# Chunk attention and a token-mixing MLP in one kernel: the hand-written order of its steps and of its loads is replaced by another

## The chip, the core and the metric

One core of a Trainium2 chip runs the whole kernel. The engines work from queues of their own and in the order of the program: PE (TensorE) multiplies and transposes, DVE (VectorE) and ACT (ScalarE) read its results out of the eight PSUM banks, POOL (GpSimd) issues the loads and SP (SyncE) nearly all stores. The time is the device time of one execution in microseconds; the median of the runs counts.

## What is computed

Inputs q, k and v have 8 batches, 8 heads, 576 tokens and 64 numbers a head. Attention stays within chunks of 64 tokens:

```python
scores = scale * np.matmul(q_c, k_c.transpose(0, 1, 2, 4, 3))
scores = scores - np.max(scores, axis=-1, keepdims=True)
attn = np.exp(scores)
attn = attn / (np.sum(attn, axis=-1, keepdims=True) + 1e-09)
out = np.matmul(attn, v_c)
```

Its result x has 512 columns for a token. The second half mixes tokens over the whole sequence of 576, with two small weight matrices, and multiplies by an output matrix of 512 x 512:

```python
wq = x @ w_q
wk = x @ w_k
W_tok = scale * np.einsum('bsd,btd->bst', wq, wk)
mixed = np.einsum('bst,btd->bsd', W_tok, x)
return np.maximum(mixed, 0.0) @ w_out
```

The kernel never forms W_tok: it computes G = wk^T x for each batch (64 x 512) and then wq G. Data in flight are float16, sums float32.

## The kernel before

The work is cut into 20 pairs of chunks, numbered 0 to 19. A whole pair is 256 tokens of one batch (two for each batch); a rest pair is the last 64 tokens of two batches together. In groups of five the numbers are: two whole pairs of an even batch, the rest pair, two whole pairs of the odd batch; so 2, 7, 12 and 17 are the rest pairs.

Each pair goes through the same steps, which the code makes as `Node`s and numbers from 0 to 592 in the order of their making:

- turn (`tq`, line 379, rest pairs line 364): PE transposes Q and K, 16 transposes for each of Q and K of a whole pair; three copies (`qkt`, line 300) bring them to the tiles `qbd` (two copies for Q) and `kt` (one for K)
- S (line 400): the score product; DVE then takes the maximum (`mx`, line 413) and subtracts it (lines 420 and 424), ACT takes the exponential (line 434, tile `es`)
- E (line 446): PE transposes the result, and a copy brings it to `et`
- V (line 477): two groups of products with v, which has a column of ones, so that the sum comes with them; DVE adds 1e-9 (`den`, line 490), takes the reciprocal (`rec`, line 494) and multiplies (line 504, tile `xs`)
- xT (line 528), pj (line 545), wkT (line 561): x transposed, projected by both small matrices, and the K half turned; copies to `xt`, `wt`, `wk` (rest pairs: `wkr`, two small copies)
- for each batch G (line 599) with two copies to `g`, mix (line 639), the relu (`rm`, lines 659 and 661), and out (line 688) with a copy to `osb`, from which a store goes to DRAM.

Copies and relu can run on ACT or on DVE; maxima, subtractions, `den`, `rec` and `xs` always run on DVE, exponentials always on ACT.

Which step stands where is not left to a scheduler. `ORDER` (line 70) is a list that lines 728 to 740 go through from left to right: `10p1` emits step 10 on PE with its result in bank 1, `11a` step 11 on ACT, `13v` step 13 on DVE, `87s` the store of step 87 on SP, `586t` a store on ACT, and `i6.256` a filler, a product of ones of 256 columns into bank 6 that nobody reads and that keeps PE occupied. Since every engine runs its part of the list in order, a step that waits holds up all that stand behind it on its engine. Banks have no other owner than the list: a PE step that takes a bank waits until the copies that read the bank's last contents are done.

`LOADS` (line 65) is the order of the loads in POOL's queue: `Q4` and `K4` are Q and K of pair 4, `v4` its v, `wqk` and `wo` the weights. Whole pairs take one transfer each for Q and K and two for v; rest pairs two for each. Pair 0 is loaded by SP as float32 and cast by ACT and DVE (steps 0 to 3). A tile for loads is one of a few buffers, so later loads also wait until earlier pairs are through (`load_more`). The constants `NQB`, `HOMES` and `LATE` and all functions are untouched by the change.

Numbers that are used below: steps 7 and 10 are the turns of Q and K of pair 0, 11 its K copy, 12 S of pair 0, 13 its maximum, 15 its exponential, 16 its E; 26 the turn of Q of pair 1, 31 S of pair 1, 91 the turn of K of pair 3; 53 the turn of rest pair 2 and 56 its K copy; 239 S of pair 8, 256 the turn of K of pair 9, 213 xT of pair 7; 551 the maximum of pair 19; 583 to 588 the last whole tile of the output in three parts, 591 and 592 the out product and the copy (and store) of rest pair 17.

Of the kernel before, what the change touches and what calls it, by code (L numbers as in the profile page):

```python
# [66 lines left out]
ORDER = """  # L70
1v 0a i7.256 i6.256 i5.256 i7.256 i6.256 i5.256 i7.256 i6.256 i5.256 i7.256 i6.256 i5.256 i7.256 i6.256 i5.256
i7.256 i6.256 i5.512 i7.256 i6.256 7p0 8v 3a 2v 6a 9a i7.512 i6.512 i5.512 i7.512 i6.512 i5.512 i7.256 10p1 11a
i7.512 i6.512 i5.512 i7.256 12p0 26p7 13v 29p6 88p5 14v 28a 27a 30a i4.512 i3.512 i2.512 i4.512 91p7 15a i6.256
31p0 92v 32v 89a i6.512 i3.512 i7.512 53p4 16p7 33v 17a 56a i3.512 i2.512 18p6 90a 54v 22p2 19v 23v 34a 24v 55v
20v 25v i1.512 i0.512 57p4 93p0 58v 35p5 21v 107p2 36a 59v 45p3 109a 94v 110p5 108a 60a i4.512 41p6 95v i2.256
61p4 111a 62a 46a i2.512 63p4 96a 37p0 64v 42v 65v 38v 43v i2.512 153p3 39v 44v 97p2 155a 40v 112p6 66v 47p0
98a 154a 113v 67p2 156p1 68a 48a i5.512 69p2 114v 157a 49p0 158p4 70v 50v 115a 159v 103p2 71p0 99p6 72a 51p0
116p1 52a 4a 172p0 117a 104v 160v 100v 175p1 73p4.5 173v 105v 174a 101v 106v 176a 102v 74v 75a 118p6 122p0 5a
78p4 161a 123v 119v 124v 125v 120v 76p2 77a 121v 126p0 199p1 79v 177p6 200a 128p2 127a 178v 162p3 202a 129a
163a 201a 130p2 179v 131a 180a 203p3 84p1 204v 82p2 205v 85a 168p6 206a 132p3 181p1 169v 83v 164p4 170v 182a  # L80
234p2 165v 133v 166v 171v 134p3.1 236a 167v 235a 183p6 136a 187p4 135a 191p2 188v 184v 189v 207p3 190v 185v
139p0 137p4 140a 192v 186v 138v 237p2 253p6 208a 238a 209p0 255a 193p7 210v 239p4 211v 194a 212v 256p2 254a
240v 213p7 195p6 214a 257v 149p0 241v 215p7 145p2 216a 196a 217p7 150v 242a 258p4 218v 302p6 259v 299p7 303a
318p3 300a 146v 86p6 301a 260v 320a 197p2 304p0 198a 243p7 319a 305v 87a 87s 244a 143p2 345p3 306v 219p6.4 348a
144a 321p7 347v 221a 220a 249p0 245p4 261a 346v 246v 250v 80p6 251v 247v 248v 322a 349p3 81a 81s 323p4 222p6
350v 223a 252v 262p2 351v 224p0 263a 324v 147p3 225a 272p6 325v 380p2 273a 383p7 352a 382v 268p4 264p0 265v
151p6 381a 266v 269v 270v 267v 384a 230p2 326a 271v 385p0 274p7 353p4 231v 307a 386v 327p2 275a 308p5 328a
276p7 354v 309a 387v 148a 148s 314p4 277a 226p2 315v 316v 152a 152s 317v 278p7 310p0 279a 333p4 227a 311v 399p6
334v 312v 335v 313v 280p7.3 402p2 336v 281v 329p0 403a 355p4 330v 228p7 337p2 401a 331v 356v 332v 357v 282a
338a 400a 358v 339p3 283p0 285p4 340v 284v 359p2 286a 341p6 232p3 360v 388a 342v 295p4 404p0 296a 343p6 361p2  # L90
405v 141p4 344a 362a 363p2 448p6 142a 142s 364v 406v 365p2.5 229a 229s 464p4 449a 233v 233s 445p7 367a 366a
407a 389p5 447v 368p2 446v 370p0 390a 369v 289p6 371a 408p5 466v 395p2 409a 391p0 376p7 392v 465a 396v 393v
397v 394v 450p4 398v 377a 290a 467p0 451v 410p2 468a 414p6 374p1 411v 412v 452v 297p0 375a 418p1 453a 413v
469p4 415v 416v 293p2 419a 417v 470v 454p1 491p3 420p6 471v 298a 298s 455a 291p7 421a 294a 493v 460p4 456p0
472a 492v 422p2 457v 458v 494v 459v 495p3 423a 287p6 461v 462v 496v 424p2 473p0 425a 497v 378p1 474a 463v 498a
475p2 288v 288s 479p4 379a 379s 526p0 480v 292a 292s 481v 426p1.6 482v 529p7 476v 427a 428v 527a 477v 429p4
478v 530a 483p6 430v 528a 431p2 499p7 432a 531p0 484v 545p4 532v 548p5 500a 546a 501p6 485p2 549a 502v 533v
439p3 547a 486a 550p4 503v 504v 534a 372p2 551v 441p6 535p0 505p1 373a 373s 442a 552v 487p2 506a 536a 507p1
488a 508v 537p4 541p6 553a 538v 542v 509p2 489p1 437p0 490v 539v 543v 440a 540v 554p1 510a 544v 511p2.3 555a
438a 438s 556p6 560p4 512v 513a 561v 564p1 557v 558v 562v 516p2 565a 435p0 559v 563v 517a 514p6 566p1 515v  # L100
433p2 567a 568p1 443p3 569a 434a 570p1 524p6 444a 444s 571v 436a 436s 572p1.7 522p0 574v 573a 525v 577p2 575p6
# [667 lines left out]
```

## Time and profile before

| | |
|---|---|
| median of 3 runs | 137.56 us (137.22 to 137.69) |
| the profiled execution | 137.94 us, of which the span from the first to the last instruction is 136.1 us |
| PE busy | 121.7 us, 89% of the span, 2120 products |
| DVE / ACT busy | 109.3 us, 80% / 100.5 us, 74% |
| granted TensorE clock | 0.994 |
| loaded and stored | 25.08 MB in 86245 packets |

An engine's row in the list of groups names its line, engine and operation, the tile written and the tile read, shapes and count; then the busy time in us and the mean of one in ns; then the idle time before the group and what ended it. A row of the timeline starts with the start time and the duration in us. A row of the waits gives the total in us, the number of waits and the longest. Busy time counts from an instruction's start to its end, and the ends of products are modelled: a product of PE begins before the end of the one ahead of it.

### The profile page before, as it was taken

Reading aid. Unit: us, or ns where it says so; the run is one execution under the profiler, and the core shown is the slowest. Engines: PE = TensorE matmul, PEld = TensorE weight load, DVE = VectorE, ACT = ScalarE, POOL = GpSimd, SP = SyncE. Lnnn points to the kernel's source line nnn. Section 1 sums busy time; section 2 is a strip of 40 time slices with the busy share of each in tenths; the row PEclk is TensorE's granted clock in tenths of the full one; section 3 lists DMA queues with packets and bytes.
Section 4 is the critical chain, followed back from the end, with each engine's and each line's share of the span. In section 5 each row is a group of like instructions: output and inputs, shape, how many; then the busy total and the mean of one; then the engine's idle time right before and its main releaser. Section 6 shows DMA issues by size and latency. Waiting matters only on the chain.

```text
span 136.1 us, 4949 instructions
## 1 busy us (share of the span) xinstructions
PE 121.7 (89%) x2120; PEld 82.6 (61%) x2120; DVE 109.3 (80%) x210; ACT 100.5 (74%) x175; POOL 74.5 (55%) x96
## 2 busy tenths in 40 slices
PE   6998879986899999999999999996999999999910
PEld 4565656865646677676668667663568766544500
DVE  5635999999898899999999979999699998636220
ACT  6358469867998777998995789865878999576600
POOL 7966989978987859995539348935600000000000
PEclk9999999999999999999999999999999999999997
DMA  3999999999999999999999999999999833619883
GB/s 85 284 180 163 172 165 172 165 168 180 174 173 171 181 175 165 175 161 245 256 176 178 281 165 152 177 242 255 202 176 225 282 76 98 154 37 250 269 256 113
DMA packets 86245, 25.08 MB, mean 184 GB/s; under 512 B 78928, under 2 KB 81744, under 8 KB 86224
## 3 DMA queue, kind: packets, MB, share of 16 engines
q0 software_dynamic: 78752, 14.29, 129.5%
q1 hardware_dynamic: 7328, 10.36, 25.7%
q8 instruction: 16, 0.26, 0.7%
q10 hardware_dynamic: 144, 0.13, 0.3%
q14 instruction: 5, 0.04, 0.1%
HBM read 29.62 MB, written 9.44 MB: 287 GB/s over the span
## 4 chain that ended last, share of the span: by engine, by line
PE 60%; DVE 13%; ACT 10%; DMA 6%; issue 5%; POOL 2%; POOLq 0%; DVEq 0%; ACTq 0%
PE ps L688 22%; PE ps L379 7%; DMA qk<-in_q_dram 6%; PE ps L528 5%; PE ps L477 5%; PE ps L400 4%; PE ps L545 4%; PE ps L639 4%; DVE xs L504 4%; PE ps L446 3%; ACT es L434 2%; DVE mx L413 2%; PE ps L599 2%; PE ps L732 2%; ACT et L300 1%
## 5 line engine op out<-in xcount | busy, mean ns | idle before, releaser
L688 PE MATMUL ps<-wo,rm 128*128 128x512 f16 (+1 forms) x148 | 35.8, 374 | 0.1
L230 POOL DMA_DIRECT2D v_all<-in_v_dram x33 | 28.7, 882 | 10.4 <-PE ps L528 4.2
L413 DVE TENSOR_REDUCE mx<-ps 128x16 f32<-128x1024 f32 (+1 forms) x20 | 22.2, 1108 | 3.0 <-PE ps L400 3.0
L504 DVE TENSOR_TENSOR xs<-ps,rec 128x512 f16<-128x512 f32 x36 | 23.9, 684 | 0.4
L434 ACT ACTIVATE es<-sh 128x1024 f16<-128x1024 f32 (+1 forms) x20 | 19.3, 972 | 1.8 <-DVE sh L424 1.7
L688 PEld LDWEIGHTS <-rm 128*128 128x128 f16 x148 | 13.1, 98 | 12.2 <-issue 0.4
L379 PE MATMUL ps<-ident,qk 128*64 128x128 f16 x512 | 19.4, 221 | 1.2 <-DMA qk<-in_q_dram 0.6
L424 DVE TENSOR_TENSOR sh<-ps,mx 128x1024 f32<-128x1024 f32 x16 | 19.6, 1224 | 0.5
L300 ACT COPY osb<-ps 128x512 f32<-128x512 f32 (+1 forms) x28 | 15.3, 574 | 4.6 <-PE ps L688 4.0
L379 PEld LDWEIGHTS <-qk 128*64 128x64 f16 x512 | 15.8, 110 | 4.5 <-DMA qk<-in_q_dram 1.3
L300 ACT COPY qbd<-ps 64x512 f32<-64x512 f32 (+1 forms) x28 | 15.7, 565 | 2.9 <-PE ps L379 1.7
L216 POOL DMA_DIRECT2D qk<-in_q_dram x15 | 13.6, 908 | 4.1 <-PE ps L379 1.6
L216 POOL DMA_DIRECT2D qk<-in_k_dram x15 | 13.5, 902 | 3.6 <-DMA qk<-in_k_dram 2.7
L661 ACT ACTIVATE rm<-ps 128x1024 f16<-128x1024 f32 (+1 forms) x12 | 13.7, 1138 | 2.0 <-PE ps L639 1.8
L300 ACT COPY et<-ps 128x512 f32<-128x512 f32 (+1 forms) x19 | 10.4, 550 | 5.5 <-PE ps L446 5.3
L732 PE MATMUL ps<-ones 128*128 128x512 f16 (+1 forms) x48 | 11.9, 383 | 1.2 <-DVE ones L155 1.2
L400 PEld LDWEIGHTS <-qbd 128*128 128x128 f16 x288 | 10.4, 98 | 3.5 <-DVE qbd L300 0.9
L446 PE MATMUL ps<-ident,es 128*128 128x128 f16 x144 | 11.2, 219 | 1.3 <-issue 1.3
L400 PE MATMUL ps<-kt,qbd 128*128 128x64 f16 x288 | 11.5, 193 | 0.7 <-DVE qbd L300 0.5
L528 PE MATMUL ps<-ident,xs 128*128 128x128 f16 x144 | 11.2, 220 | 0.9 <-DVE xs L504 0.9
L477 PE MATMUL ps<-v_all,et 64*64 64x65 f16 x576 | 10.4, 195 | 1.8 <-DVE xs L504 1.1
L477 PEld LDWEIGHTS <-et 64*64 64x64 f16 x576 | 7.8, 107 | 6.6 <-issue 2.6
(56 smaller groups left out, 177.1 us busy)
## 6 DMA issues: line engine op xcount, KB each, us to landing
out_dram<-osb SPq DMA_DIRECT2D x31, 256.0 KB, 4.5
v_all<-in_v_dram POOLq DMA_DIRECT2D x31, 128.0 KB, 6.7
qk<-in_q_dram POOLq DMA_DIRECT2D x15, 256.0 KB, 7.9
qk<-in_k_dram POOLq DMA_DIRECT2D x15, 256.0 KB, 8.0
out_dram<-osb SPq DMA_DIRECT2D x9, 128.0 KB, 4.1
v_all<-in_v_dram POOLq DMA_DIRECT2D x10, 64.0 KB, 7.8
osb<-in_q_dram SPq DMA_DIRECT2D x1, 512.0 KB, 4.1
osb<-in_k_dram SPq DMA_DIRECT2D x1, 512.0 KB, 5.1
```

The lines of the kernel that those rows point to most:

```text
L216: nc.gpsimd.dma_start(qk[u][:, t], rows)
L230: nc.gpsimd.dma_start(v_all[on, slot[u] + i, :, 0:D], v[b, :, of, :].rearrange("h p d -> p h d"))
L300: (nc.vector.tensor_copy if eng == "DVE" else nc.scalar.copy)(to, of)
L379: nc.tensor.transpose(tp[half(o), j, :, r, :], of, ident[:])
L400: nc.tensor.matmul(sp[:, i, j, c ^ turned(u, i), :], lhsT=st["qb", u][:, j, x].rearrange("p o s -> p (o s)"), rhs=st["kt", u][:, j, x * C ...
L413: nc.vector.tensor_reduce(mx[:], scores(), axis=AX.X, op=ALU.max)
L424: nc.vector.tensor_tensor(out=sh[:].rearrange("p x (g r) -> p x r g", r=R), in0=in_banks(bs, 512).rearrange("p i (x r g) -> p (i x) r g", ...
L434: nc.scalar.activation(es[:].rearrange("p x s -> p (x s)"), st["sh", u][:].rearrange("p x s -> p (x s)"), AF.Exp, scale=scale_attn,)
L477: nc.tensor.matmul(to[half(k ^ i), i if ni == 2 else w, x, :], lhsT=et[half(k), i, h // 2, h % 2, :], rhs=v_all[half(k), slot[u] + i, h, 0:W],
L504: nc.vector.tensor_tensor(out=to, in0=xp()[:, :, :, 0:D], in1=by, op=ALU.mult)
L528: nc.tensor.transpose(tx[:, f, i, :], xs[u][:, i, 2 * f : 2 * f + 2, :], ident[:])
L688: nc.tensor.matmul(in_banks(bo, wide)[:, 0], lhsT=st["rm", key][:, f, at_tok + i * P : at_tok + i * P + P], rhs=wo[:, f, s], start=(f == 0 ...
```

## The change

`LOADS` and `ORDER` are replaced as wholes; nothing else differs. Both lists hold the same 593 steps and 48 fillers (in all 18688 columns of fillers before, 17664 after). The steps' engines, banks and places differ all over the list. The beginning of the diff, with the loads, and its end:

```diff
-LOADS = "Q1 K1 Q3 K3 Q2 K2 v0 Q4 K4 v1 v2 Q5 K5 wqk v3 Q6 K6 v4 Q7 K7 wo v5 Q8 v6 K8 Q9 v7 K9 Q10 K10 Q11 Q12 K11 K12 v8 Q13 K13 v9 v10 v11 Q14 K14 v12 Q15 K15 Q16 v13 K16 v14 Q17 K17 v15 Q18 v16 K18 v17 Q19 K19 v18 v19 "
+LOADS = "Q1 K1 Q3 Q2 K2 K3 v0 Q4 v1 K4 Q5 K5 v2 wqk v3 v4 Q6 K6 Q7 K7 v5 wo v6 v7 Q8 K8 Q9 K9 Q10 K10 Q11 Q12 K12 K11 v8 Q13 v9 K13 v12 Q14 v10 v11 K14 Q15 K15 Q16 K16 v13 v14 Q17 K17 v15 Q18 v16 K18 v17 Q19 K19 v18 v19 "
...
-i7.256 i6.256 i5.512 i7.256 i6.256 7p0 8v 3a 2v 6a 9a i7.512 i6.512 i5.512 i7.512 i6.512 i5.512 i7.256 10p1 11a
-i7.512 i6.512 i5.512 i7.256 12p0 26p7 13v 29p6 88p5 14v 28a 27a 30a i4.512 i3.512 i2.512 i4.512 91p7 15a i6.256
-31p0 92v 32v 89a i6.512 i3.512 i7.512 53p4 16p7 33v 17a 56a i3.512 i2.512 18p6 90a 54v 22p2 19v 23v 34a 24v 55v
...
+i7.256 i6.256 i5.512 i7.256 i6.256 7p0 8a 3v 9a 2v i7.512 i6.512 i5.512 i7.512 i6.512 i5.512 i7.512 i6.512
+i5.256 10p0 26p1 11v 28v i7.512 i6.256 12p4 29p0 13v 88p6 30a 27a 14v i7.512 i3.512 i2.512 i7.512 31p0 53p7 32v
+56a 15a i5.512 i3.512 i2.512 i5.512 91p4 33v 54a i3.256 16p5 89a 17v 90a 55v 92a i3.512 i2.512 22p0 18p2 5v 34a
...
-523a 523s 578a 520p0 576v 518p1 521v 581p6 583p0 519a 519s 584a 584s 579p1 580v 582a 582s 589p2 587p0 585p6
-590a 591p1 586a 592v 588a 588s 592s 586t
...
+520p2 519v 589p4 581p3 521a 521s 579p2 582v 590a 591p4 580a 580s 585p5 592v 587p2 586a 586s 583p3 588v 588s
+584v 584s 592t
```

Around S of pair 8 the two lists stand like this:

```diff
-139p0 137p4 140a 192v 186v 138v 237p2 253p6 208a 238a 209p0 255a 193p7 210v 239p4 211v 194a 212v 256p2 254a
-240v 213p7 195p6 214a 257v 149p0 241v 215p7 145p2 216a 196a 217p7 150v 242a 258p4 218v 302p6 259v 299p7 303a
...
+190v 191p4 236a 140v 209p6 192a 193p5 138a 210v 253p4 211v 212v 237p2 194v 256p3 238a 254v 213p6 257a 239p0
+214a 195p5 255a 240v 215p4 196a 149p6 258p2 241v 216a 150a 217p4 145p5 218a 259v 302p4 146a 299p0 318p5 303v
```

Counted over the whole list, these steps run on DVE (the others of their kind on ACT):

| step | on DVE before | on DVE after |
|---|---|---|
| cast of pair 0 | 2 | 3 |
| clearing of g | 0 | 1 |
| Q and K copies | 15 | 12 |
| et | 1 | 4 |
| wt / wk | 4 / 5 | 2 / 2 |
| g | 5 | 7 |
| rm | 8 | 6 |
| osb | 9 | 12 |

From the maximum of pair 0 to that of pair 8 DVE has 70 steps in both lists, of which 12 before and 20 after stand directly behind the maximum, `den` or `rec` that they read; from there to the maximum of pair 19 it has 103 and 97 (21 and 18 so placed). ACT has 63 and 68 steps from its first cast to the exponential of pair 8, and 80 and 79 from there to that of pair 18.

More of the change, by code (lines that the diff above doesn't have):

```diff
@@ L64 @@
 }
-LOADS = "Q1 K1 Q3 K3 Q2 K2 v0 Q4 K4 v1 v2 Q5 K5 wqk v3 Q6 K6 v4 Q7 K7 wo v5 Q8 v6 K8 Q9 v7 K9 Q10 K10 Q11 Q12 K11 K12 v8 Q13 K13 v9 v10 v11 Q14 K14 v12 Q15 K15 Q16 v13 K16 v14 Q17 K17 v15 Q18 v16 K18 v17 Q19 K19 v18 v19 "
+LOADS = "Q1 K1 Q3 Q2 K2 K3 v0 Q4 v1 K4 Q5 K5 v2 wqk v3 v4 Q6 K6 Q7 K7 v5 wo v6 v7 Q8 K8 Q9 K9 Q10 K10 Q11 Q12 K12 K11 v8 Q13 v9 K13 v12 Q14 v10 v11 K14 Q15 K15 Q16 K16 v13 v14 Q17 K17 v15 Q18 v16 K18 v17 Q19 K19 v18 v19 "
 ORDER = """
-1v 0a i7.256 i6.256 i5.256 i7.256 i6.256 i5.256 i7.256 i6.256 i5.256 i7.256 i6.256 i5.256 i7.256 i6.256 i5.256
@@ L72 @@
-i7.256 i6.256 i5.512 i7.256 i6.256 7p0 8v 3a 2v 6a 9a i7.512 i6.512 i5.512 i7.512 i6.512 i5.512 i7.256 10p1 11a
-i7.512 i6.512 i5.512 i7.256 12p0 26p7 13v 29p6 88p5 14v 28a 27a 30a i4.512 i3.512 i2.512 i4.512 91p7 15a i6.256
-31p0 92v 32v 89a i6.512 i3.512 i7.512 53p4 16p7 33v 17a 56a i3.512 i2.512 18p6 90a 54v 22p2 19v 23v 34a 24v 55v
-20v 25v i1.512 i0.512 57p4 93p0 58v 35p5 21v 107p2 36a 59v 45p3 109a 94v 110p5 108a 60a i4.512 41p6 95v i2.256
-61p4 111a 62a 46a i2.512 63p4 96a 37p0 64v 42v 65v 38v 43v i2.512 153p3 39v 44v 97p2 155a 40v 112p6 66v 47p0
@@ L77 @@
[L77 to L81, printed above, removed]
@@ L82 @@
-139p0 137p4 140a 192v 186v 138v 237p2 253p6 208a 238a 209p0 255a 193p7 210v 239p4 211v 194a 212v 256p2 254a
-240v 213p7 195p6 214a 257v 149p0 241v 215p7 145p2 216a 196a 217p7 150v 242a 258p4 218v 302p6 259v 299p7 303a
-318p3 300a 146v 86p6 301a 260v 320a 197p2 304p0 198a 243p7 319a 305v 87a 87s 244a 143p2 345p3 306v 219p6.4 348a
-144a 321p7 347v 221a 220a 249p0 245p4 261a 346v 246v 250v 80p6 251v 247v 248v 322a 349p3 81a 81s 323p4 222p6
-350v 223a 252v 262p2 351v 224p0 263a 324v 147p3 225a 272p6 325v 380p2 273a 383p7 352a 382v 268p4 264p0 265v
@@ L87 @@
[L87 to L101, printed above, removed]
@@ L102 @@
-523a 523s 578a 520p0 576v 518p1 521v 581p6 583p0 519a 519s 584a 584s 579p1 580v 582a 582s 589p2 587p0 585p6
-590a 591p1 586a 592v 588a 588s 592s 586t
+0a 1v i7.256 i6.256 i5.256 i7.256 i6.256 i5.256 i7.256 i6.256 i5.256 i7.256 i6.256 i5.256 i7.256 i6.256 i5.256
+i7.256 i6.256 i5.512 i7.256 i6.256 7p0 8a 3v 9a 2v i7.512 i6.512 i5.512 i7.512 i6.512 i5.512 i7.512 i6.512
+i5.256 10p0 26p1 11v 28v i7.512 i6.256 12p4 29p0 13v 88p6 30a 27a 14v i7.512 i3.512 i2.512 i7.512 31p0 53p7 32v
+56a 15a i5.512 i3.512 i2.512 i5.512 91p4 33v 54a i3.256 16p5 89a 17v 90a 55v 92a i3.512 i2.512 22p0 18p2 5v 34a
@@ new lines @@
+57p5 19v 20v 58v i7.512 i6.256 107p4 23v 24v 21v i7.256 35p6 109a 25v 36a i7.256 93p2 59v 6a 41p6 4a 37p0 94v
+108a 45p5 60a 110p4 38v 39v 42v 111a 43v 44v 46a 153p4 95v i7.256 61p5 155a 112p6 40v 154a 156p2 113v 62a 157a
+i3.256 63p4 47p3 96a 114v 158p0 48a 97p2 64v 49p3 65v 98a 66v 115a 159v 67p2 99p4 50a 116p6 100v 68a 160v 117a
+69p7 70a 103p2 101v 71p7 51p6 72v 52a 104v 161a 105v 102v 73p6.7 172p0 106v 75v 118p4 173a 122p2 119v 74v 175p7
+174a 123v 124v 120v 162p6 125v 176a 76p0 121v 177p2 77a 163v 199p7 128p4 178v 201a 202a 200a 179v 129a 168p0
@@ new lines @@
+164p6 126p5 203p4 169v 127a 78p2 180a 130p5 79v 131a 170v 204v 181p2 132p5 171v 84p3 133a 182a 165v 166v 82p5
+167v 205v 187p6 83a 183p0 134p2.4 184v 206a 185v 85v 234p5 136a 186v 135a 207p4 139p2 188v 208a 189v 137p0 235a
+190v 191p4 236a 140v 209p6 192a 193p5 138a 210v 253p4 211v 212v 237p2 194v 256p3 238a 254v 213p6 257a 239p0
+214a 195p5 255a 240v 215p4 196a 149p6 258p2 241v 216a 150a 217p4 145p5 218a 259v 302p4 146a 299p0 318p5 303v
+301a 260v 197p1 143p4 300a 198a 304p6 242a 320v 345p2 305v 86p3 348a 144a 243p1 319v 346a 347a 321p4 306v 244a
@@ new lines @@
+219p2.5 322a 261a 249p0 87v 87s 245p6 349p4 250v 246v 80p3 251v 220a 247v 248v 221a 307a 262p5 252v 224p6 350v
+263a 323p0 225a 272p2 351v 147p5 324v 81a 81s 222p6 273a 383p3 325v 223a 380p2 381v 384a 268p0 264p6 230p4 265v
+382a 269v 270v 266v 271v 352a 385p2 267v 326a 151p0 386v 274p1 231a 353p6 275a 308p4 387v 327p7 309a 276p1 328a
+354v 148a 148s 310p6 314p2 152a 152s 311v 226p5 315v 312v 277a 316v 317v 278p4 313v 333p0 279a 329p2 227a 399p4
+334v 330v 331v 335v 280p6.7 336v 400a 402p5 332v 282a 401a 355p0 337p7 356v 281v 403a 339p4 357v 388a 358v
@@ new lines @@
+285p2 338v 228p5 286a 340v 295p6 283p0 296a 359p4 141p2 360a 341p4 142a 142s 229a 229s 404p2 342v 284a 361p5
+389p6 405v 232p4 362a 390v 343p5 363p7 233a 233s 448p0 364v 445p6 344a 406v 449a 365p7.1 446a 467p0 366v 367a
+464p2 407a 468v 368p4 447v 370p0 465a 369v 408p7 371a 289p6 466v 409a 395p4 391p0 396v 290a 450p2 392v 397v
+393v 376p7 394v 451v 374p6 377a 297p7 398v 375a 452v 410p4 298a 298s 414p0 293p6 415v 453a 416v 411v 417v 491p7
+412v 469p2 413v 493a 418p0 294a 492v 454p1 470v 419a 420p6 494a 291p0 421a 471v 455a 495p6 422p7 496v 472a
@@ new lines @@
+456p2 460p4 457v 287p1 458v 461v 423a 497v 473p7 459v 498a 378p6 462v 474a 463v 292a 292s 424p7 379v 379s 475p4
+425a 479p2 288a 288s 526p0 480v 476v 481v 426p6.7 482v 528a 529p1 477v 428v 427a 527a 478v 499p2 431p6 530a
+429p4 500a 485p3 432a 430v 531p0 545p2 486a 532v 548p6 547a 501p4 546a 439p3 502v 503v 533v 549a 483p2 440a
+550p6 504v 534a 372p3 551v 505p4 484a 441p0 535p5 442a 506v 487p2 552v 536a 507p4 488a 541p0 508v 537p6 553a
+509p4 489p2 538v 542v 437p5 373v 373s 539v 510a 543v 490a 554p3 544v 511p2.4 555a 540v 438a 438s 556p0 560p6
@@ L104 @@
+513a 557v 512v 435p3 561v 562v 558v 563v 564p2 516p4 559v 565a 514p6 566p2 515v 443p0 567a 517a 568p2 444v 444s
+433p1 569a 436a 570p2 524p0 434v 434s 571a 572p1.2 525v 522p3 573a 574v 575p0 523a 523s 577p4 576v 518p3 578a
+520p2 519v 589p4 581p3 521a 521s 579p2 582v 590a 591p4 580a 580s 585p5 592v 587p2 586a 586s 583p3 588v 588s
+584v 584s 592t
 """
```

## The prediction

> **What bounds the kernel now.** I read the page's head first, then busy time in three stretches, then the rows that say what each engine waits for.
>
> ```profile
> span 136.1 us, 4949 instructions
> ...
> PE 121.7 (89%) x2120; PEld 82.6 (61%) x2120; DVE 109.3 (80%) x210; ACT 100.5 (74%) x175; POOL 74.5 (55%) x96
> ...
> PE   6998879986899999999999999996999999999910
> ...
> DVE  5635999999898899999999979999699998636220
> ```
>
> PE leads over the span, but from slice 5 to slice 32 DVE stands beside it. So I cut the time at maxima (line 413) of the score steps. Stage names: mx0, mx2, mx8 and mx19 are the maxima of pairs 0, 2, 8 and 19; S8 is the score product of pair 8. Their DVE rows:
>
> ```profile
> 9.70 1.22 DVE L413 TENSOR_REDUCE mx<-ps 128x16 f32<-128x1024 f32 x1 [2.31 <-PE ps L400]
> 10.95 1.22 DVE L424 TENSOR_TENSOR sh<-ps,mx 128x1024 f32<-128x1024 f32 x1
> ...
> 18.88 0.68 DVE L413 TENSOR_REDUCE mx<-ps 128x8 f32<-128x512 f32 x1
> 19.47 0.68 DVE L504 TENSOR_TENSOR xs<-ps,rec 128x512 f16<-128x512 f32 x1
> ```
> ```profile
> 49.48 1.22 DVE L413 TENSOR_REDUCE mx<-ps 128x16 f32<-128x1024 f32 x1
> ```
> ```profile
> 108.81 1.21 DVE L413 TENSOR_REDUCE mx<-ps 128x16 f32<-128x1024 f32 x1
> ```
>
> The busy times of the three stretches between them (columns: PE, PEld, DVE, ACT, POOL, granted clock, DMA share, GB/s):
>
> ```profile
> 9.70:19.56 9.86, 8.43 (x181) 5.81 (x178) 8.32 (x14) 5.81 (x10) 8.27 (x10) 1.00 2.13 167
> 19.56:50.70 31.14, 27.70 (x591) 20.12 (x587) 29.14 (x59) 26.17 (x48) 25.95 (x32) 1.00 2.00 173
> 50.70:110.02 59.32, 57.53 (x1075) 40.65 (x1074) 55.62 (x105) 48.96 (x85) 32.29 (x39) 1.00 1.74 203
> ```
>
> In the middle one DVE is the fullest engine (29.14 of 31.14, 94%) and PE has 3.44 us idle. In the long one PE is fullest (57.53 of 59.32, idle 1.79) with DVE again at 94%. One gap makes up most of that idle time, and no semaphore explains it; it falls inside one group of eight transposes of pair 15:
>
> ```profile
> 94.85 0.27 PE L446 MATMUL ps<-ident,es 128*128 128x128 f16 x2 [1.33 <-issue]
> ```
>
> So PE and DVE set the pace together, and an order is worth what it takes out of DVE before 50 us and out of PE's waits after it. The Trainium skill (Runtime: NRT & Kernel Launch, section Instruction fetch mechanics) says that engines fetch instructions in blocks ahead of use and that this is mostly hidden. Were the gap of 1.33 us a fetch and hidden in the new order, the sum below would be 1.3 us lower; the trace does not say what the gap is, and I leave it where it is.
>
> **Early part, to mx8.** Both orders do the same steps, so each term is a count of steps that changed engine or place. The durations of those that change:
>
> ```profile
> L659 DVE TENSOR_SCALAR rm<-ps 128x1024 f16<-128x1024 f32 x7 | 9.0, 1291 | 1.1 <-PE ps L639 1.1
> ...
> L300 DVE COPY osb<-ps 128x512 f32<-128x512 f32 x9 | 6.2, 684 | 3.8 <-ACT osb L300 2.5 <-PE ps L688 1.2
> ...
> L300 DVE COPY qbd<-ps 64x512 f32<-64x512 f32 x6 | 4.1, 687 | 1.0 <-PE ps L379 0.9
> ...
> L300 DVE COPY qbd<-ps 64x256 f32<-64x256 f32 x6 | 2.5, 422 | 0.3 <-PE ps L364 0.2
> L300 DVE CAST g<-ps 64x256 f16<-64x256 f32 x5 | 2.1, 417 | 1.5 <-PE ps L599 1.4
> L300 DVE COPY xt<-ps 128x512 f32<-128x512 f32 x3 | 2.0, 669 | 0.3 <-PE ps L528 0.3
> ...
> L659 DVE TENSOR_SCALAR rm<-ps 128x512 f16<-128x512 f32 x1 | 0.7, 681 | 0.0
> ...
> L300 DVE COPY xt<-ps 128x256 f32<-128x256 f32 x1 | 0.4, 402 | 0.0
> ```
>
> From mx0 to mx8 DVE has 70 steps in both orders, and with such durations they come to 40.0 us in both. But 20 of them stand directly behind the step they read from, where 12 did. Such a neighbour starts 0.03 us after the other's end (mx0 ends at 10.92, its subtraction starts at 10.95); an independent one overlaps it by 0.09 (mx2 ends at 19.56, the next starts at 19.47). Eight more pairs at 0.12 us each add 0.9.
>
> The start itself moves. Two more 512-column fillers stand before the K turn of pair 0, the Q turn of pair 1 is put between it and S0, and its K copy goes from ACT to DVE (0.69 for 0.59):
>
> ```profile
> 6.11 1.58 PE L732 MATMUL ps<-ones 128*128 128x512 f16 x7
> ...
> 7.62 0.64 PE L379 MATMUL ps<-ident,qk 128*64 128x128 f16 x16
> ...
> 8.30 0.59 ACT L300 COPY kt<-ps 128x512 f32<-128x512 f32 x1 [0.28 <-PE ps L379]
> ```
>
> A filler costs about 0.22 (1.58 for seven, one of them half as wide). That puts the turn near 8.0 and its copy, on DVE from about 8.7 to 9.4, ahead of S0 near 9.45 and mx0 near 10.15: 0.45 later. S1 then comes earlier, because it no longer waits behind the K turn of pair 3. In ACT's queue, however, exp of pair 0 (12.21 in this profile) now stands behind the K copy of rest pair 2, whose turn follows S1; it moves to about 14.2. Behind it in that queue wait the Q copies of pairs 2 and 3; E of pair 0 waits for it, on PE. This costs E 0.3 us, since E started only at 15.02 before, and DVE finds the second maximum to do meanwhile. Counting the head of the list through, mx2 ends near 18.55, 1.0 earlier than 19.56, with 1.0 us less DVE work done by then: no net gain.
>
> From there to mx8 the extra DVE work is to be covered by DVE's idle 2.00 us. Bounds for the whole part: all of it covers (0.45 + 0.9 - 2.0 = -0.7), or none does and ACT's larger load shows as well (+2.3, below). I take **+0.5**, nearer to cover, since DVE's own idle time is the nearest row.
>
> **Loads.** Several places in the load list move (K3 behind K2, v1 ahead of K4, v2 behind K5, v4 ahead of Q6, wo behind v5, v12 ahead of Q14). POOL's queue takes the same 90 transfers, and the uses of K3, K4 and v2 move later with them. The price of a late one is one transfer's turn, 1.48 us from issue to issue (11.47 to 12.95); the whole of PE's present wait for loads, what could be gained, is 1.3:
>
> ```profile
> 11.47 0.88 POOL L216 DMA_DIRECT2D qk<-in_q_dram x1 [0.61 <-DMA qk<-in_q_dram]
> 12.95 0.88 POOL L216 DMA_DIRECT2D qk<-in_k_dram x1 [0.60 <-DMA qk<-in_k_dram]
> ```
> ```profile
> PEld L379 <- DMA qk<-in_q_dram: 1.3, 3, 0.8
> ```
>
> I take 0, inside -1.3 to +1.5; the cover is the moved use, and if it were gone PE would stand for that 1.48.
>
> **Long part, mx8 to mx19.** The new order has the K turn of pair 9 and the x transposes of pair 7 ahead of S8 instead of behind it. From the first to the next step these took 49.27 to 50.07, so PE has **0.8** less to do in this part (what it costs before S8 is in the +0.5: PE had 3.44 idle there).
>
> ```profile
> 49.27 0.64 PE L379 MATMUL ps<-ident,qk 128*64 128x128 f16 x16
> 49.84 0.40 PE L528 MATMUL ps<-ident,xs 128*128 128x128 f16 x4
> 50.07 1.03 PE L545 MATMUL ps<-xt,wqk 128*128 128x512 f16 x4
> ```
>
> DVE has 97 steps where it had 103: one large and one small rm less (1.29 + 0.68), two osb (1.37), four small qbd (1.69), one small xt (0.40) and a pair of small casts (about 0.4) less; two large qbd (1.37), one g (0.42) and one et more (0.67, by the xt row of the same shape). That is 5.83 - 2.46 = 3.4 less, and three dependent neighbours fewer (0.35). What hides this gain is PE: beside the 1.33 gap it has only 0.46 us of idle time to give back. Bounds: -2.6 (0.8 and all of 1.79) to 0. I take **-0.9**, nearest to PE's row. The banks move too, under both engines; a bank taken too soon shows as the same PE wait and is in these bounds. After mx19 the two lists hold the same steps nearly side by side: 0.
>
> **Tail.** Before, the rest pair's two stores were issued last, by SP, behind the store of another half tile:
>
> ```profile
> 129.82 0.69 DVE L300 COPY osb<-ps 128x512 f32<-128x512 f32 x1 [1.22 <-PE ps L688]
> 130.01 1.03 SPq L707 DMA_DIRECT2D out_dram<-osb x1
> 131.14 2.01 SPq L705 DMA_DIRECT2D out_dram<-osb x2
> ```
>
> SP's last issue began near 132.5, about 2.7 us after the last matmul's end (129.78). Now ACT issues these two, and the last on SP is one 256 KB store, about 0.8 after that end (copy 0.69): issued 1.9 earlier, but twice as large, and behind the same bytes on the same way out. The page's medians to landing are 4.5 us for 256 KB and 4.1 for 128. I take **-0.3**, between -1.0 and +0.6.
>
> ```profile
> out_dram<-osb SPq DMA_DIRECT2D x31, 256.0 KB, 4.5
> ...
> out_dram<-osb SPq DMA_DIRECT2D x9, 128.0 KB, 4.1
> ```
>
> **Sum:** +0.5 + 0 - 0.9 + 0 - 0.3 = -0.7 us. The profiled execution took 137.94 us (136.1 of it span), 0.38 over the median of the runs, 137.56; so I apply the difference to the median: **136.9 us**.
>
> **Rivals.** *DVE alone is the bound* (chance 0.14). Then its relief is paid in full up to PE's idle time: -2.6 in place of -0.9, 137.56 + 0.5 - 2.6 - 0.3 = 135.2. For it: DVE at 94% in two stretches. Against: PE's 1.79. The Trainium skill (Perfetto Trace Analysis, section Identifying the Most-Contended Engine) holds that matmul busy time is a poor measure and that weight-load time says how full PE is; by it PE is at 40.65 of 59.32, 69%, and DVE the bound. The trace agrees in that PE's groups reach past the start of the next (49.27 + 0.64 is past 49.84), which can hide short waits in the 97%.
>
> *ACT's queue takes DVE's place* (0.36), the slower side. Up to the exp of pair 8 ACT has 68 steps for 63, 2.3 us more by such counts (three large and one small Q/K copy, two wk, two wt, a small rm and an osb more; two et, a g, a clear and a cast less).
>
> ```profile
> L300 ACT COPY qbd<-ps 64x512 f32<-64x512 f32 x26 | 15.0, 580 | 2.7 <-PE ps L379 1.7 <-DVE qbd L300 0.6
> ...
> L300 ACT COPY et<-ps 128x512 f32<-128x512 f32 x16 | 9.3, 586 | 5.3 <-PE ps L446 5.0
> ...
> L300 ACT CAST wk<-ps 128x256 f16<-128x256 f32 x5 | 1.9, 373 | 1.2 <-PE ps L561 1.1
> ```
>
>  Place: 19.56 to 50.70, where ACT had 4.97 us idle; it decides once the extra copies stand ahead of an exp or et that PE waits for, as with exp of pair 0. Half of it exposed, the long part unable to give it back: 137.56 + 0.5 + 1.15 - 0.3 = 138.9, and 138.6 with a third of the 0.9 kept. For it: two us of delay at the first exp. Against: the long part has 0.5 us less ACT work.
>
> *The edit does nothing that shows* (0.14): PE's own steps, identical in both, set the time from S8 on, and early delays and gains cancel: 137.5.
>
> **Numbers.** The forecast, 136.9, has 0.36, with its own range 136.2 to 137.5. No change is within 0.3% (0.41 us: 137.15 to 137.97), about what a measurement can tell. Faster: 0.14 + 0.33 = 0.47. Same: 0.03 of the forecast and 0.10 of the last rival, 0.13. Slower: 0.36 + 0.04 = 0.40. The range for 8 in 10, over both signs and the bounds: 135.1 to 139.0.
>
> **What would show it.** Right: mx0 near 10.15, exp of pair 0 near 14.2, mx8 ending at 50.0 to 52.0, mx8 to mx19 shorter by 0.5 to 1.5, last store issued within 1.2 us of the last matmul's end. Wrong: ACT over 90% busy between mx2 and mx8 with PE waiting for exp or et; a new PE wait for a load; or PE idle for more than 1.8 us between mx8 and mx19.

## The result, and the profile after

| | before | after |
|---|---|---|
| median of 20 runs each, side by side | 137.37 us (136.26 to 138.19) | 136.41 us (136.05 to 137.09) |
| ratio after / before, 95% interval | | 0.9934 (0.9912 to 0.9956) |
| the profiled execution, its span | 137.94 us, 136.1 us | 136.40 us, 134.3 us |

The kernel became faster by 0.66%, with an interval that leaves out both no change and a gain of one per cent. Here and below, a ratio leaves out the runs of either kernel that took over 1.5% longer than its fastest, while medians and ranges are of all runs. The forecast was 136.9 us. Part of the trace answers as it said, but the terms of the sum do not all come out as it had them. First the head of the page after, with the rows of PE and DVE over 40 slices:

```profile
span 134.3 us, 4948 instructions
...
PE 120.3 (90%) x2120; PEld 82.1 (61%) x2120; DVE 109.8 (82%) x210; ACT 99.7 (74%) x175; POOL 74.4 (55%) x96
...
PE   6898896987879999999999999999999999999910
...
DVE  4558999999989989999989839999997998855520
```

In the first slices PE looks as before; from slice 13 on it is full. The marks mx0, mx2, mx8 and mx19, in DVE's order of time (start, us, engine, line, operation, tiles, shapes), and between mx0 and mx2 the exponential of pair 0 in ACT's:

```profile
10.17 1.23 DVE L413 TENSOR_REDUCE mx<-ps 128x16 f32<-128x1024 f32 x1
...
17.46 0.64 DVE L413 TENSOR_REDUCE mx<-ps 128x8 f32<-128x512 f32 x1
```
```profile
13.86 1.06 ACT L434 ACTIVATE es<-sh 128x1024 f16<-128x1024 f32 x1
```
```profile
49.55 1.22 DVE L413 TENSOR_REDUCE mx<-ps 128x16 f32<-128x1024 f32 x1 [0.37 <-ACT xt L300]
```
```profile
106.92 1.22 DVE L413 TENSOR_REDUCE mx<-ps 128x16 f32<-128x1024 f32 x1
```

So mx8 ends at 50.77 (before 50.70) and mx19 at 108.14 (before 110.02). The whole gain of the trace lies between them. The three stretches again (PE, PEld, DVE, ACT, POOL, granted clock, DMA share, GB/s):

```profile
10.17:18.10 7.93, 6.98 (x143) 4.51 (x141) 7.20 (x11) 5.24 (x9) 7.18 (x10) 1.00 2.18 165
18.10:50.77 32.67, 28.79 (x632) 21.86 (x627) 30.69 (x62) 26.95 (x49) 26.56 (x33) 1.00 1.98 171
50.77:108.14 57.37, 56.26 (x1061) 39.39 (x1057) 52.13 (x100) 50.79 (x91) 32.35 (x40) 1.00 1.79 211
```

The long part took 57.37 us where it took 59.32: 1.95 less, of which PE's idle time gives only 0.68 (1.79 to 1.11). To see where the time is gained, compare the moments at which PE has done the same amount of work in the two kernels, which is nearly independent of the order of steps. Worked out from the start and the usual length of every PE step, as lead (minus) or lag (plus) against before, at the time that before had there (good to some 0.3 us, because different steps are done at the same moment):

```
before at (us)      27.7   36.8   52.0   65.1   83.8   90.2   98.0  113.9  128.6
after              -0.25  -0.94  -0.74  -0.66  -0.57  -0.28  -2.05  -1.84  -1.87
```

A lead of 0.74 at S8 (the 0.8 us of moved PE work) is worn down to 0.28 by 90 us. Then, within 8 us, it jumps to 2.05, and little more happens to the end. At moments when both lists have done exactly the same PE steps, the lead is 0.36 us (at 91.0) and 1.84 to 1.87 (from 114 on): the jump is really 1.48. Its place is the gap in the transposes of pair 15, and so is its size: the two transposes beside the gap start 1.55 us apart before, where neighbours start 0.06 apart, so the gap costs PE 1.49 us. In the kernel after, the same group of eight runs through:

```profile
92.40 0.61 PE L528 MATMUL ps<-ident,xs 128*128 128x128 f16 x8
92.85 0.61 PE L446 MATMUL ps<-ident,es 128*128 128x128 f16 x8
93.33 0.61 PE L528 MATMUL ps<-ident,xs 128*128 128x128 f16 x8
```

At the tail nothing is gained. PE's last matmul, the copy, and the queues of ACT and SP that issue the last stores (rows of one answer):

```profile
126.99 1.89 ACTq L705 DMA_DIRECT2D out_dram<-osb  x2
127.15 0.42 DVE L300 COPY osb<-ps 128x256 f32<-128x256 f32 x1 [0.18 <-DMA out_dram<-osb]
127.32 2.61 SPq L707 DMA_DIRECT2D out_dram<-osb  x3
127.95 0.69 DVE L300 COPY osb<-ps 128x512 f32<-128x512 f32 x1 [0.38 <-PE ps L688]
```

The last matmul ended at 127.92, 1.86 earlier than before (129.78), and the span's end (134.28) followed 6.37 us later, where it was 6.36 (136.14).

### The profile page after: what moved, and what is told of

It is laid out like the page before. It is cut to its first block, busy times and chain, and to the rows that moved or that the text cites. A ratio compares the mean times of both kernels' runs of the same rounds, so it can differ in the third digit from the quotient of the medians.

```text
span 134.3 us, 4948 instructions
## 1 busy us (share of the span) xinstructions
PE 120.3 (90%) x2120; PEld 82.1 (61%) x2120; DVE 109.8 (82%) x210; ACT 99.7 (74%) x175; POOL 74.4 (55%) x96
## 4 chain that ended last, share of the span: by engine, by line
PE 44%; DVE 20%; DMA 12%; ACT 10%; issue 5%; POOL 4%; POOLq 0%; DVEq 0%; ACTq 0%
PE ps L688 15%; DMA qk<-in_q_dram 12%; DVE mx L413 5%; PE ps L528 5%; PE ps L639 4%; PE ps L379 4%; DVE xs L504 4%; PE ps L446 4%; PE ps L545 4%; DVE sh L424 4%; PE ps L477 3%; POOL qk L216 3%; PE ps L400 3%; ACT es L434 2%; ACT rm L661 2%
## 5 line engine op out<-in xcount | busy, mean ns | idle before, releaser
L300 ACT COPY osb<-ps 128x512 f32<-128x512 f32 (+1 forms) x25 | 14.3, 581 | 6.8 <-PE ps L688 6.7
L300 ACT COPY qbd<-ps 64x512 f32<-64x512 f32 (+1 forms) x31 | 16.6, 538 | 3.7 <-PE ps L379 3.3
L661 ACT ACTIVATE rm<-ps 128x1024 f16<-128x1024 f32 (+1 forms) x14 | 15.5, 1117 | 0.7 <-PE ps L639 0.7
L300 ACT COPY kt<-ps 128x512 f32<-128x512 f32 (+1 forms) x17 | 9.1, 540 | 5.9 <-PE ps L379 3.7
L732 PE MATMUL ps<-ones 128*128 128x256 f16 (+1 forms) x48 | 10.9, 361 | 1.2 <-DVE ones L155 1.2
L477 PE MATMUL ps<-v_all,et 64*64 64x65 f16 x576 | 9.9, 195 | 1.9 <-ACT qbd L300 0.7
L300 DVE COPY osb<-ps 128x512 f32<-128x512 f32 (+1 forms) x12 | 8.0, 663 | 4.4 <-PE ps L688 4.2
```

Source lines behind the costliest of these rows:

```text
L300: (nc.vector.tensor_copy if eng == "DVE" else nc.scalar.copy)(to, of)
L477: nc.tensor.matmul(to[half(k ^ i), i if ni == 2 else w, x, :], lhsT=et[half(k), i, h // 2, h % 2, :], rhs=v_all[half(k), slot[u] + i, h, 0:W],
L661: nc.scalar.activation(to, of, AF.Relu, scale=scale_moe)
```

## The experiments

The question was what the jump is, since it holds most of the gain. Theory A: it is the old gap, which comes from a bunch of stores and loads ahead of it and not from what the engines have to compute. Theory B: it is the new order's own work, less on DVE and other places on PE. Some expectations give the letters to rivals of their own and say so. The runs came in three groups of four, each beside runs of the kernel before on the same chip (medians 137.49, 137.56 and 137.45).

**The kernel before, again.** Is the gap there each time?

> The kernel before, unchanged, profiled a second time. The question is the gap of 1.33 us inside the transposes of pair 15 (at 93.5 us of the first profile), which no semaphore explains and which the profile of the new order does not have. Theory A (the long part from mx8 to mx19 shrank by 1.95 us because of the order: less work on DVE and 0.8 us less on PE): the gap is there again within 1 us of its place, and the part takes 59.0 to 59.6 us. Theory B (most of the 1.95 is this gap, which comes and goes from one execution to the next): the gap is gone or elsewhere, and the part takes 57.8 to 58.3 us.

One run, 137.86 us, span 136.1; from mx8 to mx19 59.03 us, the low end of the range that this expectation gave its own Theory A. The gap stands at the same place, inside the same group, but is shorter, 0.78 for 1.33:

```profile
93.45 0.49 PE L444 MATMUL ps<-ident,es 128*128 128x128 f16 x6
94.72 0.27 PE L444 MATMUL ps<-ident,es 128*128 128x128 f16 x2 [0.78 <-issue]
```

The place belongs to the program, the length does not. (Line numbers are smaller by 2 in the experiments' kernels.)

**One half of the new lists at a time.** The old head and old loads before the new list's last 402 entries, and the reverse; the seams lie in the order around S8:

```diff
 e2: old head, new rest
-... 240v 215p4 196a 149p6 258p2 241v 216a 150a 217p4 ...
+... 149p0 241v 215p7 196a 258p2 216a 150a 217p4 ...
 e3: new head, old rest
-... 139p0 137p4 140a 192v 186v 138v 237p2 253p6 208a 238a 209p0 ...
+... 137p0 235a 190v 191p4 236a 140a 192v 138v 237p2 253p6 238a 209p0 ...
```

> The old list and old load order up to the small projection of rest pair 7 (the 74th step of PE, about 51 us), then the new list for all that is left. Theory A (the gain lies behind mx8; the first 50 us end level, 50.70 and 50.77): as fast as the new kernel, 0.991 to 0.996 of the kernel before. Rival (the new head leaves banks, buffers and queues in a better state, and the rest lives on that): 0.997 to 1.003.

> The new list and new load order up to the Q copy of pair 8 behind the x transposes of pair 5 (the 64th step of PE, about 44 us), then the old list for the rest. Theory A: no gain, 0.998 to 1.003 of the kernel before. Rival (the head makes the gain): 0.990 to 0.996.

The old head with the new rest took 137.25 us (136.98 to 137.98), ratio 1.0002 (0.9973 to 1.0031); the new head with the old rest 138.07 (137.01 to 141.42), ratio 1.0027 (0.9995 to 1.0059). Neither half gains alone: e2 came out as its rival had it, e3 as its theory. But both seams cost time of their own: in e2 the stretch from the maximum of pair 9 to that of pair 10 takes 4.46 us for 3.71 in the kernel after, and in e3 PE goes from some 0.3 ahead of before at 43.7 us to 0.64 behind at 48.8. So neither run measures what a head is worth, and that stays open. What they show is the gap: it is absent with the new rest and present with the old one. In e3 (whose profiled execution, 141.42 us, was the longest of its runs) it is 3.02 us long, in the same group of eight. e2 first, then e3:

```profile
94.00 0.61 PE L444 MATMUL ps<-ident,es 128*128 128x128 f16 x8
```
```profile
93.64 0.44 PE L444 MATMUL ps<-ident,es 128*128 128x128 f16 x5
97.09 0.48 PE L444 MATMUL ps<-ident,es 128*128 128x128 f16 x3 [3.02 <-issue]
```

**The new load order alone, in the old list.**

```diff
-LOADS = "Q1 K1 Q3 K3 Q2 K2 v0 Q4 K4 v1 v2 Q5 K5 wqk v3 Q6 K6 v4 Q7 K7 wo v5 ...
+LOADS = "Q1 K1 Q3 Q2 K2 K3 v0 Q4 v1 K4 Q5 K5 v2 wqk v3 v4 Q6 K6 Q7 K7 v5 wo v6 ...
```

> The old list of steps with the new order of loads. Theory (loads pay or cost only where PE waits for them, before 30 us; K3 then lands 1.5 to 2 us after its use in the old list, K4 and v2 likewise about 2 us): slower by 1 to 2 us in the early part, of which later idle time takes back a part, 1.003 to 1.015. Rival (the new load order is itself the gain, whatever the list): 0.99 to 0.997.

140.83 us (139.41 to 142.15), ratio 1.0146 (1.0084 to 1.0209), as the theory had it. PE's lag against before is 0.95 at 18.9 us and 2.11 at 27.7, and then constant until 90 us: all of it is lost while the first pairs wait for their loads. The cover that the prediction named, the uses of K3, K4 and v2 that move later together with their loads, is real, and it is worth 2.1 us: without it the load order alone costs more than the whole change gains.

**What the gap is.** PE's own instructions come over a DMA queue of their own, 16 transfers of 16 KB; the page of before shows them only as a sum:

```profile
q8 instruction: 16, 0.26, 0.7%
```

0.26 MB in 16 transfers, for PE's 4,240 matmuls and weight loads; no other engine has more than 262 instructions in the trace. In the DMA records of the traces each transfer has a start. For the twelfth, the one next to the gap, with the number of PE's instructions that had begun by then (its 20 or so others counted in), and how long PE then stood idle:

```
kernel              start us   landed   PE instructions   idle us  PE goes on
after                 88.93    89.81         3125          none
old head (e2)         90.32    91.21         3125          none
late stores, SP (e10) 91.31    92.24         3197          none
late stores (e5)      91.40    92.29         3205          0.13       93.86
before                92.41    93.37         3249          1.33       94.85
before again (e1)     92.48    93.44         3247          0.78       94.72
new loads (e4)        93.93    94.89         3241          0.60       96.22
new head (e3)         94.78    95.73         3265          3.02       97.09
```

Where the transfer starts while PE is at instruction 3197 or earlier, PE does not stand; where it starts at 3205 or later, it does. In the other six traces of the new list the start lies at 3121 to 3133, and PE does not stand there. In all five cases PE stops at the same point, with 3265 instructions begun, and goes on 1.3 to 1.6 us after the transfer has landed (94.85 - 93.37 = 1.48; 1.28; 1.33; 1.36; 1.57 in e5), however long it stood. So the gap is an instruction fetch that came late. The Trainium skill (Runtime: NRT & Kernel Launch, section Instruction fetch mechanics) calls the cost of crossing into a new block mostly hidden; in the kernel after it is, and in these five runs it is not, by 0.13 to 3.02 us.

What makes the fetch late? SP's queue just ahead of it, before, and then after:

```profile
81.88 6.88 SPq L711 DMA_DIRECT2D out_dram<-osb  x6
93.49 1.13 SPq L705 DMA_DIRECT2D out_dram<-osb  x2
```
```profile
78.96 5.74 SPq L711 DMA_DIRECT2D out_dram<-osb  x6
90.95 1.13 SPq L705 DMA_DIRECT2D out_dram<-osb  x2
```

Six stores of 256 KB leave SP in both. In the old order they start 2.9 us later, and their last issue ends at 88.76 (after: 84.70), close to where the fetch is due (88.93 in the kernel after, which is not held up).

**Only that, in the old order.** Stores 229 and 233 are issued behind 298 instead of ahead of it. No other entry moves.

```diff
-448p6 142a 142s 364v 406v 365p2.5 229a 229s 464p4 449a 233v 233s 445p7 ...
-298a 298s 455a ...
+448p6 142a 142s 364v 406v 365p2.5 229a 464p4 449a 233v 445p7 ...
+298a 298s 229s 233s 455a ...
```

> The kernel before with one edit: the stores of steps 229 and 233 (four transfers of 256 KB, issued at 84 to 89 us) stand behind the store of step 298 in SP's queue, so they go out after 93.5 us. Theory A (the gap in pair 15's transposes is a late fetch of PE's instructions: its 16 KB packet, due near 89 us, starts 3 us late because six stores and seven loads were issued between 82 and 89): the packet starts on time, the gap is gone, the runs spread less, and the kernel takes 136.2 to 136.7, 0.990 to 0.996 of the kernel before. Theory B (the new order's gain is DVE's and PE's work moved, the gap a bystander): 0.998 to 1.004.

136.75 us (136.15 to 137.56), ratio 0.9951 (0.9921 to 0.9981), as Theory A expected. SP now issues two stores there and the others behind the fetch, and the transposes of pair 15 come in one row:

```profile
82.09 2.00 SPq L709 DMA_DIRECT2D out_dram<-osb  x2
93.70 1.13 SPq L703 DMA_DIRECT2D out_dram<-osb  x2
94.88 0.62 SPq L709 DMA_DIRECT2D out_dram<-osb  x1
```
```profile
93.24 0.89 PE L444 MATMUL ps<-ident,es 128*128 128x128 f16 x8
```

PE is 0.21 behind before until 90 us and 0.99 ahead from 98 us to the end: two places in SP's queue are worth 1.2 us of PE, and 0.5% of the time where the whole change gives 0.66%. That is the gap and nothing else, since the transposes beside it now start 0.35 us apart instead of 1.55.

Two things did not come as Theory A had them. A rest of the gap is still there: the row takes 0.89 us, where the same eight transposes take 0.61 in the kernel after. And the packet did not start on time. PE came to instruction 3125 at 88.87 us before, at 88.85 after and at 89.09 here, and the transfer started 3.54, 0.08 and 2.31 us later. So the moved stores make 1.2 us of the delay, which is just enough; where the other 2.3 come from was not tested. In the seven us ahead of that instruction POOL issued eight loads before and here, and six in the kernel after.

**The new order with the old engines.** 24 of its copies and relu go back to the engine that they had before.

```diff
-150a 218a 146a 303v 320v 319v 346a 347a 87v 381v 382a 231a 338v 360a 284a 390v ...
+150v 218v 146v 303a 320a 319a 346v 347v 87a 381a 382v 231v 338a 360v 284v 390a ...
```

> The new order and loads, but the 24 copies and relu between mx8 and mx19 that run on the other engine than before are given back to their old engine (2.1 us more on DVE, 2.1 less on ACT). Theory A (the gain is the fetch that is on time; DVE's relief pays nothing): within 0.3 us of the new kernel, 136.2 to 136.7, 0.991 to 0.996. Theory B (DVE's relief pays in the long part): 1 to 2 us slower than the new kernel, 0.998 to 1.006.

142.75 us (142.54 to 142.97), ratio 1.0376 (1.0328 to 1.0424): worse than either theory had it. DVE has 2.1 us more to do and the kernel loses 6.3. The first loss shows how. The relu of rest pair 2 (step 150), the small copies of rest pair 7 (218) and a copy of an output tile (146) stand on DVE behind a subtraction of 1.23 us:

```profile
50.76 1.23 DVE L422 TENSOR_TENSOR sh<-ps,mx 128x1024 f32<-128x1024 f32 x1
...
51.90 0.68 DVE L657 TENSOR_SCALAR rm<-ps 128x512 f16<-128x512 f32 x1
...
52.49 0.44 DVE L298 CAST wkr<-ps 64x64 f16<-64x64 f32 x2
...
52.99 1.08 PE L377 MATMUL ps<-ident,qk 128*64 128x128 f16 x32 [0.83 <-DVE wkr L298]
...
54.84 0.64 PE L377 MATMUL ps<-ident,qk 128*64 128x128 f16 x16 [0.77 <-DVE osb L298]
```

PE's next turns take the banks that these copies empty. In the kernel after they stand on ACT, are done when PE comes, and PE runs on without a wait. (Because 24 steps moved at once, the run does not price any of them; the three of the next run are among them.)

```profile
51.47 0.43 ACT L300 CAST wkr<-ps 64x64 f16<-64x64 f32 x2
...
52.15 1.53 PE L379 MATMUL ps<-ident,qk 128*64 128x128 f16 x48
52.26 0.58 ACT L300 COPY osb<-ps 128x512 f32<-128x512 f32 x1 [0.36 <-PE ps L688]
```

**Three copies more on DVE.** To part DVE's load from the place in its queue, three copies of output tiles, from which only a store reads, go from ACT to DVE: 2.05 us.

```diff
-302p4 146a 299p0 ... 274p1 231a 353p6 ... 363p7 233a 233s
+302p4 146v 299p0 ... 274p1 231v 353p6 ... 363p7 233v 233s
```

> The new kernel with three copies of output tiles (2.05 us in all) moved from ACT to DVE, at the same steps of the list. Theory A (what counts is where an urgent copy stands in an engine's queue; these copies are urgent for nobody): 136.2 to 136.8 us, ratio 0.991 to 0.996. Rival B (DVE's load bounds the long part): the 2.05 us come back in full, 137.5 to 138.6 us, ratio 1.000 to 1.008.

138.36 us (137.95 to 138.99), ratio 1.0111 (1.0085 to 1.0136); the kernel after beside it: 136.32. The number is Rival B's, 2.0 us for 2.05, but the trace does not show an engine that is full. PE loses in three jumps of 0.75, 0.79 and 0.54 us, each at one of the copies. The first:

```profile
52.24 1.22 DVE L411 TENSOR_REDUCE mx<-ps 128x16 f32<-128x1024 f32 x1
53.37 0.68 DVE L298 COPY osb<-ps 128x512 f32<-128x512 f32 x1
```
```profile
54.10 0.64 PE L377 MATMUL ps<-ident,qk 128*64 128x128 f16 x16 [0.58 <-DVE osb L298]
```

The copy, which ACT began at 52.26, now waits behind a maximum until 53.37, and the turn of pair 11 waits for its bank. The second is of the same kind. The third is not: there the copy holds up the two small copies behind it in DVE's queue, and those PE waits for:

```profile
83.39 0.68 DVE L298 COPY osb<-ps 128x512 f32<-128x512 f32 x1
83.99 0.46 DVE L298 CAST wkr<-ps 64x64 f16<-64x64 f32 x2
```
```profile
84.51 0.30 PE L597 MATMUL ps<-xs,wkr 128*64 128x256 f16 x2 [0.34 <-DVE wkr L298]
```

The run's premise, that these copies are urgent for nobody, was wrong: nobody is in a hurry for the tile, but PE is for the bank, or for what stands behind. DVE was idle 5.58 of 59.46 us (91% busy) in this long part. The run therefore does not part load from order; it shows that in this order each of the three steps sits on PE's path, two through their bank and one through the queue.

**The tail.** Four kernels change only the last stores: the kernel after with rest pair 17's two stores on SP (e7); with the half tiles last, their stores on ACT (e8) or on SP (e11); and the late stores of e5 with all last stores on SP (e10).

```diff
 e7, from the kernel after
-586s 583p3 588v 588s 584v 584s 592t
+586s 583p3 588v 588s 584v 584s 592s
 e8, from the kernel after
-591p4 580a 580s 585p5 592v 587p2 586a 586s 583p3 588v 588s 584v 584s 592t
+583p6 580a 580s 591p4 584v 584s 585p5 592a 592s 587p2 586v 588a 588t 586t
 e11, from the kernel after: as e8, but the end is
+586v 586s 588a 588s
 e10, from e5
-586a 592v 588a 588s 592s 586t
+586a 592v 588a 586s 588s 592s
```

> The new kernel with one edit at the end: the two stores of rest pair 17 are issued by SP, behind all others, and not by ACT. The theory of the tail (an issue on SP costs 0.5 to 1.3 us there, and moving two of them to ACT saves what the larger last store then costs): 1.0 to 1.8 us slower than the new kernel, 137.4 to 138.2. Rival (what ends last is the traffic, 1.8 MB of stores in the last 9 us, and who issues them is nothing): within 0.3 us of the new kernel.

> The new kernel with another tail: the 512-column tile of pair 19 (step 583) is computed before the out product of rest pair 17 and the two half tiles come last; their stores of 128 KB go out on ACT, the rest on SP. If issue time on SP and the size of the last store set the end: 0.5 to 1.2 us faster than the new kernel, 135.2 to 135.9. Rival (traffic): within 0.3 us of it.

> The new kernel unchanged, so that the three others have it beside them on one chip. Expected 136.0 to 136.7 us, ratio to before 0.990 to 0.996; no idle time of PE inside the transposes of pair 15, and the long part (end of maxima 8 to end of maxima 19) 57.0 to 57.8 us.

> The kernel before with two edits of the queues' lists and nothing else: the two stores of SP's queue put behind the next ones, as in the run with late stores, and all of the last stores issued by SP. Theory A (the gain of the new order is the gap inside the transposes of pair 15, which the stores in front of the instruction fetch make; and issues from SP and ACT at once slow each other): 135.9 to 136.5 us, ratio 0.987 to 0.993, as good as the new kernel without its order. Rival B (the end gains nothing from issuing on SP alone in this list): as the run with late stores, 136.6 to 137.0 us, ratio 0.993 to 0.997. Rival C (the new order's own work counts): not under 137.0 us.

> The new kernel with the half tiles computed last and all last stores issued by SP. If both the size of the last store and the issuing queue set the end: 135.2 to 135.7 us, ratio 0.981 to 0.987. Rival: only the issuing queue counts, then as the run with the last stores on SP: 135.7 to 136.0 us, ratio 0.986 to 0.990; issues of SP 0.5 to 0.7 us each in both cases.

| kernel | median us (range) | ratio to before (95% interval) |
|---|---|---|
| after, again (e9) | 136.32 (136.07 to 136.96) | 0.9919 (0.989 to 0.9947) |
| after, last stores on SP (e7) | 135.76 (135.62 to 137.92) | 0.9868 (0.9822 to 0.9915) |
| after, half tiles last, ACT (e8) | 136.76 (136.0 to 138.64) | 0.9943 (0.9906 to 0.998) |
| after, half tiles last, SP (e11) | 136.19 (136.03 to 136.37) | 0.9904 (0.9869 to 0.9939) |
| late stores, last on SP (e10) | 136.57 (136.02 to 137.81) | 0.9959 (0.9922 to 0.9995) |

Half tiles at the end gained nothing, whoever issued the stores: e8 and e11 lie outside what either side expected of them. e7 went against its theory: without ACT's help at the end the kernel is not slower. Its median is the lowest of all, and four of its six runs lie below every run of the kernel after; but its interval overlaps that of e9, which ran in another group, so a gain over the kernel after is likely and not settled. Its profiled execution has 0.2 us of its lead by 25 us already, where the edit reaches nothing; 0.31 is the tail (last matmul at 127.71, end 6.06 us later; in e9, the kernel after again, 6.25). SP's issues in it, and then in e11:

```profile
127.12 2.31 SPq L705 DMA_DIRECT2D out_dram<-osb  x3
129.48 1.13 SPq L703 DMA_DIRECT2D out_dram<-osb  x2
```
```profile
128.06 2.52 SPq L703 DMA_DIRECT2D out_dram<-osb  x2
130.67 1.02 SPq L705 DMA_DIRECT2D out_dram<-osb  x2
```

The theory behind e10 and e11 was that issues from SP and ACT at once slow each other. In the kernel after, ACT's second issue took 1.31 us and SP's beside it 1.26, where issues before that took 0.54 to 0.62. The Trainium skill (Perfetto Trace Analysis, section DMA Instruction — HWDGE (DVE, Sync)) says that the issuing engines share one block that makes the descriptors and is locked for one at a time, and that the wait for the lock counts as the issue's time; these two rows agree. But e11 has an issue of 1.58 us with SP alone, e10 one of 1.35, and e7 none over 0.95; the kernel before already has one of 1.37 (the first of its two at 131.14), 1.4 us after the end of ACT's only issue. So another queue is not needed for a long issue, the theory does not hold as stated, and e10 gained nothing that shows over e5 (136.57 for 136.75; its ratio is the one that Rival B expected). e9 fell within all that was expected of it.

## Why the prediction came out right, point by point

- **The total** (136.9, own range 136.2 to 137.5) holds, and so does the sign. Beneath it, the early and the long part came out 0.4 and 1.05 us faster than their terms and the tail 0.3 slower. On the profiled pair, from which the terms were taken, they add up to -1.87 us where the forecast had -0.7, and the span shrank by 1.86. The total holds because the median moved by only 0.96 (last point below), and that is luck.
- **Early part, +0.5.** Measured +0.07 (mx8 ends at 50.77 for 50.70). The start moved as worked out: mx0 0.47 later (0.45 forecast), the exponential of pair 0 at 13.86 (14.2), mx2's end at 18.10 (18.55). The eight further dependent neighbours (0.9) were covered better than the value taken had it.
- **Loads, 0.** Among the waits of the kernel after, those for Q of PE's turns have grown, 2.3 us for 1.3 (a second row, for K, which the prediction left out of "the whole" of this wait, is 0.8 for 0.4):

```profile
PEld L379 <- DMA qk<-in_q_dram: 2.3, 3, 1.1
```

  That is the new PE wait named as a sign against the forecast; but mx8 comes only 0.07 later with 0.8 us more of PE's work done, so it cost nothing on balance. e4 puts a price on the cover: 2.1 us, where the prediction had one transfer's turn, 1.48.
- **Long part, -0.9.** Measured -1.95: this is the term that was mis-sized. Its 0.8 for PE's moved work is there (0.74 of lead at S8). What failed is the choice on the gap of 1.33 us, "I leave it where it is". The sentence beside it, that the sum would be 1.3 lower if the gap were a fetch and hidden in the new order, describes what happened in the profiled execution: PE's lead grows by 1.48 us there, and e5 reproduces 1.2 of it by moving two stores. The relief of DVE brought nothing that shows: 3.49 us less busy (counted: 3.4), and 1.54 more idle (5.24 for 3.70). Of the lead of 0.74 on PE, 0.38 was even lost again by 91 us.
- **Tail, -0.3.** Measured +0.01. The last store was issued 1.45 us after the last matmul's end, not 0.8, because SP's issue ahead of it took 1.26; it landed 5.16 after it, where before that was 5.14. e7, which gives the two issues back to SP, shows no loss.
- **The rivals.** DVE was not the bound in the sense of the first one: 91% busy in the long part, and its relief not paid out; the rule on weight-load time in the Trainium skill (Perfetto Trace Analysis, section Identifying the Most-Contended Engine), by which it would have been the bound, would have put the time 1.2 us too low (135.2 for 136.41). ACT did not take its place: 26.95 of 32.67 us from mx2 to mx8, 82%, under the 90% named. "Nothing shows" is excluded by the interval.
- **The median gained less (0.96 us) than the profiled execution (1.54).** The kernel before scatters by 1.9 us beside the kernel after and by about 4 in its other groups (136.08 to 140.51 in the first), the kernel after by 1.0 (136.05 to 137.09). With PE standing 0.13 to 3.02 us in five traces of the old rest of the list, a fetch that is late by chance would make such a scatter; how much of it was not measured, since the other runs have no traces. It does not make all of it: in e10's profiled execution PE did not stand, and it took 137.76 us, over a microsecond more than the median of its runs; and e8's (138.64, the new list, with the fetch on time) had fallen 2.16 us behind e9's by S of pair 5, where PE waits for loads of Q.

## What to carry to other kernels

When PE stands still inside a group of matmuls with "issue" as the cause and no semaphore behind it, look for its instruction transfers among the DMA records and for stores and loads in the microseconds ahead of them; here, moving two stores behind the transfer gave 1.2 of the 1.5 us back and cost nothing that shows. When a copy is moved between engines, ask first which matmul takes its bank next and what stands ahead of it in the new queue: the length of the copy says less than that. Here a load order and the order of its uses were one edit: the new loads without their list cost PE 2.1 us.
